# RWKV-6 attention and a Gelu MLP on one core: three of four additions into g made by accumulating transfers, with new slot plans

## The chip, the cores and the metric

The kernel runs on one core of a Trainium2 chip. The metric is device time in microseconds of one execution; several executions are taken, and their median stands for the kernel. A profile of one execution goes with it.

## The reference, cut to what matters

```python
# attention (rwkv6_finch): batch 4, heads 8, 768 steps, head size 48
for t in range(S):
    cur = einsum('bhd,bhe->bhde', u[None] * kt, vt)
    y[:, :, t] = einsum('bhd,bhde->bhe', rt, state + cur)
    state = wt[:, :, :, None] * state + einsum('bhd,bhe->bhde', kt, vt)
# MLP on x = y as (3072 tokens, 384)
h = x @ w_in                       # 384 -> 2048
g = 0.5 * h * (1 + erf(h / sqrt(2)))
out = g @ w_out                    # 2048 -> 384
```

Everything is f32. The weights arrive as 64-bit floats and are converted on the chip.

## The kernel before

The tokens are cut into eight blocks x = 0 to 7 of 384 tokens. For each block `attention(x, ...)` makes the 384 x 384 tile xT (features by tokens), and `mlp(x)` makes 384 rows of the output from it. The main loop runs eight turns: in turn x the MLP of block x - 1 is interleaved with the attention of block x (turn 0 has only attention, for two halves of the heads, and conversion of weights), and a last `mlp(7)` runs alone.

The order is written by hand through generators. Each stream yields between steps, and a string of `PLAN[x]` says which stream goes next: "." the MLP, "s" the attention, "f" the first step of the attention after it, "l" the loads of the next block (issued by SP), "c" the conversion of weights, "x" sums of xT, "w" masks and sums of weights, "p" preparation. All engines get their instructions in that order, and each engine runs its own in order; semaphores tie them together. In this way a long f32 matmul stream of the MLP keeps TensorE (PE) busy while VectorE (DVE), ScalarE (ACT) and DMAs work on the attention.

For x > 0 of the MLP, the product h = xT by w_in is made by `h_halves()` in a form with seven products of halves (as Strassen's and Winograd's scheme does) in place of eight. The hidden features go in HK = 4 turns q; each turn has the steps `first` to `seventh`. A step calls `two(o, q, ...)`, which issues two or four f32 matmuls of 128x192 into a PSUM bank (a matmul is two passes in the profile); `first`, `fifth` and `sixth` issue two, `second`, `third`, `fourth` and `seventh` four. What else they do:

- `first` copies its PSUM bank into a second one (L972, ACT), `second` goes on adding to the first.
- `second` and `fourth` end in a Gelu straight from PSUM (L961, ACT).
- `fifth` and `sixth` copy their PSUM into the tile g, for the quarters (1, 1) and (0, 1) of turn q (L992 and L996, ACT).
- `third` and `seventh` save their PSUM in the SBUF tile o_sb (L965, ACT; two buffers) and add it to what lies in g (L983 and L1001, DVE). A Gelu in place on g follows later (`gelu(q, 0, 1, ...)` and `gelu(q, 1, 1, ...)`; L961, for even blocks of the MLP L958 and L961, since 64 of the columns go to the tile `alone`).

The order in a turn q > 0 is first(q), third(q-1), seventh(q-1), second(q), fifth(q), sixth(q), fourth(q-1); after the last turn come seventh(3), third(3), and fourth(3) with the last Gelus, during the first product of the second matmul (`rest`). Then `of_g` (L921 to L925) makes sums of blocks of g on DVE, and `product` (L1068) multiplies by w_out in the same scheme.

Of the attention, the lines named later are L452 (products of k and r in blocks 0 and 1, PE), L505 and L494 (updates of r and k, DVE), L579 and L588 (the same products in later blocks), L711 (kv_ps, PE), L726 (the chain of states on DVE, which reads kv_ps), L752 (y_ps, PE), L897 (sums of xT), L385 (products of k and r on DVE), L163 and L204 (a memset of one column ahead of a load, so that the load waits for its buffer). GpSimd (POOL) sets up masks and tiles in the first microseconds and has no instruction of the kernel after that.

Of the kernel before, what the change touches and what calls it, by code (L numbers as in the profile page):

```python
# [18 lines left out]
ALU = mybir.AluOpType  # L19
# [17 lines left out]
NC_SP = 8  # L37
HALFWAY = 2
PLAN = {
    0: ".lls.....sslsc.lsslll.sl.sls..sl.lscsl..sss.lscs.lscs.s.clll.s..s.pcsss...wss..sccs.ffp",  # L40
    1: (
        "c.c.csc.cc.ccc.sscwllsc.cwccccs.wc.csscwc.cccc.s.slwccccc.ccs.cwc.ccw.cs.cscccccsccs.s..cc"
        "slcs.ccl.ss.lccsclccsc.lc.c..lwfws..ffwf.swf.f.xxw.x.f...lxx"
    ),
    2: (
        "w.ssws.l...swl.w.s.....ws....ssl.wwl.ws.slwsss.slsws..s.s......s.s.sss.s.ss...s..s...s..ls"
        "sl.lsfsff..s.flf...xx.fxfxx"
    ),
    3: (
        ".s...ls....s...s.ss...s.lsssss.s..ssls.ss...sss..ssssls.s...s...ls....lssl.slssl.fs..lffs."  # L50
        ".ffx.x..xxx"
    ),
    4: (
        "ss.ss...l.....ss..s..s...sss..ssss..ssll...ll.s.ss....sss....sss.ssl..s..s...s.ssll.s.lfsf"
        "..sf.ff..xx..xfxlx"
    ),
    5: (
        "ssl.s..l......ss.s..s...s.ssssss.s.s.s.ss...sss..lssslss.....ss.s.s....ls..lllssslfs..flsf"
        ".f..fx.x.xxx"
    ),  # L60
    6: (
        "ss....s...s.sls..s...s.l...sss.sllss..s.sss.l...s..s..ssslsss.s...ss....s....ss.lssl..lfsf"
        "f..fs..f.x.x.lxfxfx"
    ),
    7: ".s....s...s....sss...s.ssss.ssss.s..ss...sss..ssssss.s......s.s...s.s.sss..s..x..x.xxx",
}


# [5 lines left out]
def kernel(  # L74
# [9 lines left out]
    nc = tc.nc  # L84
# [32 lines left out]
    def bank_u(i):  # L117
        return pools["u"].tile([128, BANK], F32, name="u_ps", tag=f"u{i % 2}")

    def bank(name="o_ps"):  # L120
        return ps.tile([128, BANK], F32, name=name, tag="mm", bufs=2)
# [146 lines left out]
    for i, h in enumerate(QUARTERS[:1]):  # L268
        for a in range(3):
            w_q = (3 - a) * C // 4  # L270
            z = q_ints[1 if a == 0 else 2]
# [582 lines left out]
    HK = HF // 2  # L854
# [45 lines left out]
    def mlp(x):  # L900
# [14 lines left out]
        def of_g(k):  # L915

            s1.append(s12_of["s1"][k])
            s2.append(s12_of["s2"][k])
            s3.append(s3_sb[0][:, k * FG:(k + 1) * FG])
            a00, a10, a11 = (gs[g][:, :, a:a + 128] for g, a in ((k, 0), (k, 128), (k + 2, 128)))  # L920
            nc.vector.tensor_add(s1[k], a10, a11)  # L921
            yield
            nc.vector.tensor_sub(s2[k], s1[k], a00)
            yield
            nc.vector.tensor_sub(s3[k], a00, a10)  # L925
            yield

        def multiply(o, lhsT, rhs, start=False):
            nc.tensor.matmul(o, lhsT=lhsT, rhs=rhs, start=start, stop=True, skip_group_check=True)  # L929
# [3 lines left out]
        def h_halves():  # L933

            x00, t1, x10, x11, l0, l1 = (xT[:, c, b * HT:(b + 1) * HT] for c in range(3) for b in range(2))
            t2, t3, t4, l01 = x_sums

            def w(a, c):
                return lambda f: w_in_sb[:, (a * HF + f) // FI, c, f % FI * 128:(f % FI + 1) * 128]

            def s(i):
                return w(1, 0) if i == 1 else lambda f: s_of[i - 2][f // FI][:, f % FI * 128:(f % FI + 1) * 128]

            def two(o, q, *factors, start=False):
                for i in range(2):
                    for n, (lhs, rhs) in enumerate(factors):
                        multiply(o[:, i * HT:(i + 1) * HT], lhs(2 * q + i), rhs, start and i == n == 0)

            def of_two(o):
                return o.rearrange("p (f t) -> p f t", f=2)  # L950

            def g_of(q, a, b):
                return gs[2 * a + 2 * q // FG][:, 2 * q % FG:2 * q % FG + 2, b * HT:(b + 1) * HT]

            def gelu(q, a, b, z):
                o = g_of(q, a, b)
                if waits and b:
                    nc.scalar.activation(out=o[:, :, 0:256 - HT], in_=z[:, :, 0:256 - HT], func=AF.Gelu)  # L958
                    f = a * HF + 2 * q
                    o, z = alone[:, f:f + 2], z[:, :, 256 - HT:]  # L960
                nc.scalar.activation(out=o, in_=z, func=AF.Gelu)  # L961

            def saved(o):
                z = wk.tile([128, DM], F32, name="o_sb", bufs=2)
                nc.scalar.copy(out=z, in_=o)  # L965
                return of_two(z)

            def first(q):
                a_of[q] = h_bank()
                two(a_of[q], q, (w(0, 0), x00), start=True)  # L970
                u_of[q] = bank_u(q)[:, 0:2 * HT]
                nc.scalar.copy(out=u_of[q], in_=a_of[q])  # L972

            def second(q):
                two(a_of[q], q, (w(0, 1), x10), (w(0, 2), l0))
                gelu(q, 0, 0, of_two(a_of[q]))
                if q:
                    gelu(q - 1, 0, 1, g_of(q - 1, 0, 1))

            def third(q):  # L980
                two(z_of[q], q, (s(4), x11), (w(0, 2), l1))
                z = saved(z_of[q])
                nc.vector.tensor_add(g_of(q, 0, 1), g_of(q, 0, 1), z)  # L983

            def fourth(q):
                two(u_of[q], q, (w(1, 1), t4), (w(1, 2), l01))
                gelu(q, 1, 0, of_two(u_of[q]))

            def fifth(q):
                z_of[q] = h_bank()  # L990
                two(z_of[q], q, (s(1), t1), start=True)
                nc.scalar.copy(out=g_of(q, 1, 1), in_=of_two(z_of[q]))  # L992

            def sixth(q):
                two(u_of[q], q, (s(2), t2))
                nc.scalar.copy(out=g_of(q, 0, 1), in_=of_two(u_of[q]))  # L996

            def seventh(q):
                two(u_of[q], q, (s(3), t3), (w(1, 2), l1))
                z = saved(u_of[q])  # L1000
                nc.vector.tensor_add(g_of(q, 1, 1), g_of(q, 1, 1), z)  # L1001

            def h_bank():
                return bank("h_ps")[:, 0:2 * HT]

            a_of, z_of, u_of = {}, {}, {}
            for group in (0, 2, 1, 3):
                gs[group] = gp.tile([128, FG, T], F32, name="g")
            for q in range(HK):
                first(q)  # L1010
                yield
                if q:
                    third(q - 1)
                    yield
                    seventh(q - 1)
                    yield
                else:
                    fifth(q)
                    yield
                second(q)  # L1020
                yield
                if q:
                    fifth(q)
                    yield
                sixth(q)
                yield
                if q:
                    fourth(q - 1)
                    gelu(q - 1, 1, 1, g_of(q - 1, 1, 1))
                    yield  # L1030
            q = HK - 1
            seventh(q)
            yield
            third(q)
            for _ in of_g(0):
                pass
            yield

            def rest():
                fourth(q)  # L1040
                gelu(q, 0, 1, g_of(q, 0, 1))
                gelu(q, 1, 1, g_of(q, 1, 1))
            late[:] = [rest]
# [3 lines left out]
        if fast:  # L1047
            yield from h_halves()
# [47 lines left out]
        if halves:  # L1096
# [29 lines left out]
            for c in range(2):  # L1126
                z = o_sb[1][:, c * HM:(c + 1) * HM]
# [40 lines left out]
        elif ends:  # L1168
# [16 lines left out]
            for c in range(2):  # L1185
                z = o_sb[1][:, c * HM:(c + 1) * HM]
# [126 lines left out]
```

## Time and profile before

| | |
|---|---|
| median of 3 runs | 595.2 us (593.16 to 595.92) |
| profiled execution, its time | 593.95 us |
| profiled execution, its span | 592.2 us |
| PE, matmul | 573.1 us, 97% of the span |
| DVE | 443.9 us, 75% |
| ACT | 290.0 us, 49% |
| POOL | 8.0 us, 1% |
| HBM read and written | 36.24 and 4.72 MB |
| transfers of SP's and ACT's queue (q1) | 50,832 packets, 45.62 MB, 25.5% of 16 engines |
| additions into g on DVE (L983, L1001) | 56, 549 and 548 ns each |
| granted TensorE clock | 0.994 |

Times are in microseconds from the start of the span unless marked ns. The span runs from the first to the last instruction; the execution's own time is 1.75 us longer. A busy share is an average over stages; the attention's first block and the last MLP alone have other limits than the turns between. A line of the profile names the source line, the engine, the operation, the tiles (written <- read), the shape and the count.

### The profile page before, as it was taken

The page shows a single profiled execution, that of the slowest core. Times are in us where ns is not written, and L with a number is a line of the kernel's source. Part 1 is how long each engine was busy: PE and PEld are TensorE (multiplying, and loading weights), DVE is VectorE, ACT ScalarE, POOL GpSimd, SP SyncE. Part 2 cuts the span into 40 slices and gives each one's busy share as a digit, 9 for nine tenths or more (in the row PEclk, how much of TensorE's full clock was granted, in tenths as well). Part 3 has the DMA queues.
Part 4 walks back from the last instruction along what each step waited for, and adds up shares of the span by engine and source line. Part 5 has one row for each costly group of instructions (what it writes and reads, how often), then busy time and mean ns, then how long its engine had stood idle before and what let it go on. Part 6 is the DMA issues. An engine that isn't in the chain of part 4 may idle for free.

```text
span 592.2 us, 17602 instructions
## 1 busy us (share of the span) xinstructions
PE 573.1 (97%) x7602; PEld 522.3 (88%) x7616; DVE 443.9 (75%) x867; ACT 290.0 (49%) x668; POOL 8.0 (1%) x21
## 2 busy tenths in 40 slices
PE   6789999999999999999999999999999999999998
PEld 3576666699999999999999999999999999999997
DVE  6877976999959986787859987598859988521432
ACT  2259998235552556146552456345560467235400
POOL 3100000000000000000000000000000000000000
PEclk8989999999999999999999999999999999999999
DMA  6659652031032401431023301441013200110000
GB/s 236 201 192 311 226 186 85 19 120 56 1 65 68 130 5 34 116 122 37 2 43 103 121 19 22 112 138 55 1 32 92 72 2 12 31 45 1 1 14 34
DMA packets 51005, 46.82 MB, mean 79 GB/s; under 512 B 31728, under 2 KB 36080, under 8 KB 50928
## 3 DMA queue, kind: packets, MB, share of 16 engines
q1 hardware_dynamic: 50832, 45.62, 25.5%
q8 instruction: 60, 0.98, 0.7%
q14 instruction: 17, 0.14, 0.1%
q10 hardware_dynamic: 96, 0.07, 0.1%
HBM read 36.24 MB, written 4.72 MB: 69 GB/s over the span
## 4 chain that ended last, share of the span: by engine, by line
PE 62%; DVE 3%; SPq 1%; DMA 1%; issue 0%; ACT 0%; DVEq 0%
PE o_ps L1068 24%; PE h_ps L929 16%; PE u_ps L929 14%; PE d L588 4%; DVE st L726 2%; PE y_ps L752 1%; PE y_ps L797 1%; PE kv_ps L711 1%; SPq L531 1%; PE d L579 1%; DMA rkw<-in_rkw_dram 0%; DMA rkw<-kx 0%; DVE kx L385 0%; PE u_ps L588 0%; DVE f L1133 0%
## 5 line engine op out<-in xcount | busy, mean ns | idle before, releaser
L929 PE MATMUL h_ps<-xT,w_in_sb 128*128 128x192 f32 x560 | 111.0, 330 | 0.1
L929 PEld LDWEIGHTS h_ps<-xT,w_in_sb 128*128 128x128 f32 x560 | 93.0, 190 | 3.7 <-ACT g L961 1.4
L929 PE MATMUL u_ps<-s,w_in_sb 128*128 128x192 f32 x224 | 41.1, 326 | 0.0
L1068 PE MATMUL o_ps<-w_out_sb,g 128*128 128x192 f32 x224 | 39.8, 326 | 0.0
L929 PEld LDWEIGHTS u_ps<-s,w_in_sb 128*128 128x128 f32 x224 | 37.1, 190 | 0.1
L1068 PEld LDWEIGHTS o_ps<-w_out_sb,g 128*128 128x128 f32 x224 | 37.0, 190 | 0.0
L604 ACT COPY a_sb<-d 32x256 f32<-32x256 f32 (+8 forms) x90 | 32.7, 363 | 4.0 <-PE d L588 2.5
L726 DVE SCALAR_TENSOR_TENSOR st<-st,tot_sb,kv_ps 128x48 f32<-128x48 f32 x160 | 29.1, 258 | 5.3 <-PE kv_ps L711 5.2
L452 PEld LDWEIGHTS d<-rkw 64*64 64x64 f32 x1152 | 19.5, 137 | 15.3 <-issue 9.3
L1054 PE MATMUL h_ps<-xT,w_in_sb 128*128 128x384 f32 x96 | 32.6, 492 | 0.0
L823 ACT COPY ysb<-y_ps 128x384 f32<-128x384 f32 x8 | 3.8, 480 | 57.8 <-PE y_ps L797 28.8
L1068 PE MATMUL o_ps<-w_out_sb,f 128*128 128x192 f32 x176 | 32.0, 330 | 0.0
L1068 PE MATMUL o_ps<-t,e 128*128 128x192 f32 x176 | 31.2, 328 | 0.0
L1068 PE MATMUL o_ps<-w_out_sb,e 128*128 128x192 f32 x176 | 31.2, 328 | 0.0
L1068 PE MATMUL o_ps<-t,s 128*128 128x192 f32 x176 | 31.2, 328 | 0.0
L983 DVE TENSOR_TENSOR g<-g,o_sb 128x384 f32<-128x384 f32 x28 | 15.4, 549 | 20.9 <-ACT o_sb L965 20.9
L1068 PE MATMUL o_ps<-t,g 128*128 128x192 f32 x176 | 31.0, 330 | 0.0
L452 PE MATMUL d<-rkw 64*64 64x64 f32 (+1 forms) x1152 | 22.2, 224 | 7.5 <-DMA rkw<-in_rkw_dram 3.0
L1068 PEld LDWEIGHTS o_ps<-w_out_sb,f 128*128 128x128 f32 x176 | 28.7, 190 | 0.4
L1068 PEld LDWEIGHTS o_ps<-t,g 128*128 128x128 f32 x176 | 28.6, 190 | 0.5
L1068 PEld LDWEIGHTS o_ps<-t,e 128*128 128x128 f32 x176 | 28.8, 190 | 0.2
L1068 PEld LDWEIGHTS o_ps<-t,s 128*128 128x128 f32 x176 | 28.8, 190 | 0.2
(163 smaller groups left out, 1187.4 us busy)
## 6 DMA issues: line engine op xcount, KB each, us to landing
rkw<-in_rkw_dram SPq DMA_DIRECT2D x54, 256.0 KB, 3.7
raw<-in_w_out_dram SPq DMA_DIRECT2D x8, 768.0 KB, 4.8
v_in<-in_v_dram SPq DMA_DIRECT2D x8, 584.0 KB, 4.3
raw<-in_w_in_dram SPq DMA_DIRECT2D x5, 768.0 KB, 6.6
out_dram<-o_sb SPq DMA_DIRECT2D x20, 192.0 KB, 1.9
rkw<-kx SPq DMA_DIRECT2D x72, 48.0 KB, 2.0
rkw<-in_rkw_dram SPq DMA_DIRECT2D x6, 384.0 KB, 5.7
raw<-in_w_in_dram SPq DMA_DIRECT2D x9, 256.0 KB, 4.7
```

Of the source, the lines that this page charges most:

```text
L452: nc.tensor.matmul(d[half[p], g, n * width:(n + 1) * width], lhsT=kc[half[g], b, i, p], rhs=right(half[g], b, i, p), start=True, stop=True)
L531: dma.dma_start(out=block_of_kt(dst, src), in_=kb[src * 32:(src + 1) * 32, dst])
L579: nc.tensor.matmul(fine_of(d, g)[half[p], a * n_b:], lhsT=places[half[g], a, p * C:(p + 1) * C], rhs=fine_sb[half[g], 0:FINE - a, a], star ...
L588: nc.tensor.matmul(o[half[p], i * 3 * C // 2:(i + 1) * 3 * C // 2], lhsT=kc[half[g], n // NI, n % NI, p], rhs=rx[half[g], 2 * n + p], star ...
L604: nc.scalar.copy(out=at[z, g, first:behind, (a + 1) * h:], in_=d[z, :, :, to] if g == slice(None) else d[z, :, to])
L711: nc.tensor.matmul(kv_ps[half[g], p, i * D:(i + 1) * D], lhsT=k_t(b, i, p, g), rhs=vs(b, i, g)[half[p], 0:D], start=True, stop=True)
L726: nc.vector.scalar_tensor_tensor(out=stq[:, q, c], in0=stq[:, q, c - 1] if c else b4[:, q, NC - 1], scalar=totq[:, q, c:c + 1], in1=kvs[q ...
L752: nc.tensor.matmul(y[p][half[g ^ swap(b)], i * C:(i + 1) * C], lhsT=vs(b, i, g)[half[p]], rhs=at[half[p], g, b * NI + i, :], start=(i == 0 ...
L929: nc.tensor.matmul(o, lhsT=lhsT, rhs=rhs, start=start, stop=True, skip_group_check=True)
L983: nc.vector.tensor_add(g_of(q, 0, 1), g_of(q, 0, 1), z)
L1054: nc.tensor.matmul(h_ps, lhsT=w_in_sb[:, f // FI, j, f % FI * 128:(f % FI + 1) * 128], rhs=xT[:, j, :], start=(j == 0), stop=(j == NJ - 1))
L1068: nc.tensor.matmul(o, lhsT=lhs(j), rhs=rhs(j), start=start and j == 0, stop=(j == HF - 1), skip_group_check=True)
```

## The change

Three things are changed. First, for the turns q = 0, 1 and 2 of `h_halves` the addition of o_sb to g is no longer a DVE instruction but a DMA from o_sb to g with an accumulating operation, issued by GpSimd; for q = 3 DVE adds as before. With seven blocks in this form these are 42 transfers (128 partitions, two rows of 192 f32 each, 192 KB) and 14 additions. Second, the Gelus of these quarters are issued later: `gelu(q-1, 0, 1)` moves from second(q) to behind fourth(q-1), and `gelu(q-1, 1, 1)` from behind fourth(q-1) to behind third(q) of the next turn, or behind seventh(3) after the last. Third, all eight strings of `PLAN` are new; they hold other orders of the same streams. Below, two of the eight strings are shown.

```diff
 PLAN = {
-    0: ".lls.....sslsc.lsslll.sl.sls..sl.lscsl..sss.lscs.lscs.s.clll.s..s.pcsss...wss..sccs.ffp",
+    0: ".s...sl.ll.lclsllllssssl.lsl.l.ssl.lls..ssssc..s.sclcs.s..s..s.s.ss.s..csps.s.s.fpcfw",
...
-    7: ".s....s...s....sss...s.ssss.ssss.s..ss...sss..ssssss.s......s.s...s.s.sss..s..x..x.xxx",
+    7: "ss.ss.....s..s..s....s.ssss.ss...ss.s.ss..sss..sssss..s..s...s..s..s.s.sss..s.x..x..xxx",
 }
...
             def second(q):
                 two(a_of[q], q, (w(0, 1), x10), (w(0, 2), l0))
                 gelu(q, 0, 0, of_two(a_of[q]))
-                if q:
-                    gelu(q - 1, 0, 1, g_of(q - 1, 0, 1))
+
+            def add_to(q, z, g):
+                if q < HK - 1:
+                    nc.gpsimd.dma_start(out=g, in_=z, accum_op=ALU.add)
+                else:
+                    nc.vector.tensor_add(g, g, z)
 
             def third(q):
                 two(z_of[q], q, (s(4), x11), (w(0, 2), l1))
-                z = saved(z_of[q])
-                nc.vector.tensor_add(g_of(q, 0, 1), g_of(q, 0, 1), z)
+                add_to(q, saved(z_of[q]), g_of(q, 0, 1))
...
             def seventh(q):
                 two(u_of[q], q, (s(3), t3), (w(1, 2), l1))
-                z = saved(u_of[q])
-                nc.vector.tensor_add(g_of(q, 1, 1), g_of(q, 1, 1), z)
+                add_to(q, saved(u_of[q]), g_of(q, 1, 1))
...
                 if q:
                     third(q - 1)
+                    if q > 1:
+                        gelu(q - 2, 1, 1, g_of(q - 2, 1, 1))
                     yield
                     seventh(q - 1)
                     yield
...
                 if q:
                     fourth(q - 1)
-                    gelu(q - 1, 1, 1, g_of(q - 1, 1, 1))
+                    gelu(q - 1, 0, 1, g_of(q - 1, 0, 1))
                     yield
             q = HK - 1
             seventh(q)
+            gelu(q - 1, 1, 1, g_of(q - 1, 1, 1))
             yield
             third(q)
```

More of the change, by code (lines that the diff above doesn't have):

```diff
@@ L39 @@
 PLAN = {
-    0: ".lls.....sslsc.lsslll.sl.sls..sl.lscsl..sss.lscs.lscs.s.clll.s..s.pcsss...wss..sccs.ffp",
+    0: ".s...sl.ll.lclsllllssssl.lsl.l.ssl.lls..ssssc..s.sclcs.s..s..s.s.ss.s..csps.s.s.fpcfw",
     1: (
-        "c.c.csc.cc.ccc.sscwllsc.cwccccs.wc.csscwc.cccc.s.slwccccc.ccs.cwc.ccw.cs.cscccccsccs.s..cc"
-        "slcs.ccl.ss.lccsclccsc.lc.c..lwfws..ffwf.swf.f.xxw.x.f...lxx"
-    ),
-    2: (
-        "w.ssws.l...swl.w.s.....ws....ssl.wwl.ws.slwsss.slsws..s.s......s.s.sss.s.ss...s..s...s..ls"
-        "sl.lsfsff..s.flf...xx.fxfxx"
-    ),
-    3: (
-        ".s...ls....s...s.ss...s.lsssss.s..ssls.ss...sss..ssssls.s...s...ls....lssl.slssl.fs..lffs."
-        ".ffx.x..xxx"
-    ),
-    4: (
-        "ss.ss...l.....ss..s..s...sss..ssss..ssll...ll.s.ss....sss....sss.ssl..s..s...s.ssll.s.lfsf"
-        "..sf.ff..xx..xfxlx"
-    ),
-    5: (
-        "ssl.s..l......ss.s..s...s.ssssss.s.s.s.ss...sss..lssslss.....ss.s.s....ls..lllssslfs..flsf"
-        ".f..fx.x.xxx"
-    ),
-    6: (
-        "ss....s...s.sls..s...s.l...sss.sllss..s.sss.l...s..s..ssslsss.s...ss....s....ss.lssl..lfsf"
-        "f..fs..f.x.x.lxfxfx"
+        "cs.c.cc.sslclcc.cs..ccswcc.sswccc.cccs.c.cccss.ccc.sc.scwlcclcsc.css.cs.clscsscclccc.sclls"
+        "lc.wcc.ccfcccf.cc.s...fc.wcc.swcc.cc...cf.w.wwwx.xwxf.wl.f.xx"
+    ),
+    2: (
+        "sw..sl..wss.....s..sws....ssw.wsw.sw.w.ss.lss..s.sw.ll.sw.s...ssls.s.s.ls..ss.s....s...sss"
+        ".lsll.f.s.fs.ff..x.xl.xfxx"
+    ),
+    3: (
+        "l.s.s..s...sls.ss....s...s.sss.ss.ss.ss...s.ssss..sssssssll....s....l..sl.sssls..llsf..sf."
+        "ff.x.l.x.xfxx"
+    ),
+    4: (
+        "sss...s..l....sl.s..s.s...l.ss..sss.l.s.s.ss.s.s...s.sl.ssl...sssss..s.....s.s..lss.sllfsf"
+        "..lfs.f.f.x.x.xfxx"
+    ),
+    5: (
+        ".ss...sss.l.....ss....sl.sssslss.s......sslss.sss..sssss..s..sl..s..s...s.lslsll.ssf.ff.s."
+        ".x..x.lxxx"
+    ),
+    6: (
+        "lls...ssss.s.s.s......l.s.s....s..sss.ssss.ss..sll..s...s..s..sss.s.sl.ss..s....slss.sl.lf"
+        ".sf.f.s.ff..xx.xfxlx"
     ),
-    7: ".s....s...s....sss...s.ssss.ssss.s..ss...sss..ssssss.s......s.s...s.s.sss..s..x..x.xxx",
+    7: "ss.ss.....s..s..s....s.ssss.ss...ss.s.ss..sss..sssss..s..s...s..s..s.s.sss..s.x..x..xxx",
 }
```

## The prediction

> **What bounds the kernel now.** I read the page's first two parts, the engines' busy time by stage, the waits of TensorE, the waits of all engines, ACT's and PE's timeline in one turn of the loop that is edited, and the DMA issues. The page first:
>
> ```profile
> PE 573.1 (97%) x7602; PEld 522.3 (88%) x7616; DVE 443.9 (75%) x867; ACT 290.0 (49%) x668; POOL 8.0 (1%) x21
> ```
>
> PE is the bound. A busy PE need not be a dense one, so I also looked at the pitch: in the timeline 12 passes of 128x192 take 1.95 us, 0.1625 us each, in all stages after 50 us. A tighter order has nothing to win there; only idle time can go. By stage (columns: stretch, its length, then busy time of PE, PEld, DVE, ACT, POOL, the clock, the DMA share, GB/s):
>
> ```profile
> 0.00:50.00 50.00, 37.36 (x1089) 27.19 (x1102) 36.92 (x113) 21.80 (x37) 8.02 (x21) 0.93 0.66 213
> ...
> 258.00:330.00 72.00, 71.63 (x871) 69.12 (x869) 59.12 (x113) 33.16 (x83) 0.00 (x0) 1.00 0.20 53
> 330.00:394.00 64.00, 63.67 (x832) 60.80 (x832) 51.90 (x97) 32.54 (x84) 0.00 (x0) 1.00 0.28 79
> ```
>
> In the two loops shown PE idles 0.37 and 0.33 us; of the 19.1 us of idle time in the span 12.6 lie in the first 50 us. DVE is busy for 52 to 59 us of those loops, but that is work beside PE. Which waits does it end? The waits of PE, in full for all that matters:
>
> ```profile
> PE d L452 <- DMA rkw<-in_rkw_dram: 3.0, 1, 3.0
> PE d L452 <- issue: 2.3, 2, 1.5
> PE warm L225 <- ACT zeros L217: 2.3, 1, 2.3
> PE y_ps L752 <- DVE st L726: 2.1, 5, 0.7
> PE kv_ps L711 <- issue: 2.0, 1, 2.0
> PE kv_ps L711 <- ACT kx L687: 1.1, 2, 0.9
> PE d L452 <- DVE rkw L505: 0.7, 1, 0.7
> PE d L452 <- DVE rkw L163: 0.4, 1, 0.4
> PE warm L225 <- issue: 0.3, 1, 0.3
> PE u_ps L929 <- DVE s L897: 0.3, 1, 0.3
> PE warm L225 <- DVE raw L204: 0.2, 1, 0.2
> ```
>
> Waits that DVE ends are 2.1 + 0.7 + 0.4 + 0.3 + 0.2 = 3.7 us. That is all that a freer DVE and better slots can give back, unless they also shorten a wait that no instruction of the program ends ("issue").
>
> **What is removed.** 42 of the 56 additions on DVE:
>
> ```profile
> L983 DVE TENSOR_TENSOR g<-g,o_sb 128x384 f32<-128x384 f32 x28 | 15.4, 549 | 20.9 <-ACT o_sb L965 20.9
> L1001 DVE TENSOR_TENSOR g<-g,o_sb 128x384 f32<-128x384 f32 x28 | 15.3, 548 | 7.1 <-ACT o_sb L965 6.9
> ```
>
> 42 x 0.549 = 23.1 us of DVE work, six additions or 3.3 us in each of seven loops. The row's last part says that DVE stood idle for 28 us ahead of them, so it had the time. On the path it is worth little: the largest wait that DVE ends, y_ps behind the state chain of L726 (2.1 us), comes after matmuls that make kv_ps, and DVE itself waits for these ("DVE st L726 <- PE kv_ps L711", 5.2 us in 8 waits). The chain of 16 or 20 such operations starts when kv_ps is there, however free DVE was before. I keep those 2.1 us, and the 0.3 of the x sums.
>
> **What is moved.** All loops have other slots. The matmuls are the same in kind and count (3,840 in both programs, two passes each where f32), and in both orders PE changes 122 times between 64-row and 128-row tiles, so PE's work is the same sum. In loop 0 the first instructions of the weight and x loads (the one-column memsets of L163 and L204) stand in other places of DVE's order: five of L163 now stand together ahead of the second updates. I count the waits of loop 0 behind L505 and L163 (0.7 + 0.4) as gone, 1.0 us rounded. In loop 1 the attention's matmuls come some slots earlier and the Gelu products later; PE is 99% busy there (70.98 of 72 us) with either first. SP's loads move with the slots; DMA share is 0.2 to 0.28 in the later loops, so I cost that at nothing; were a load late, the attention's first step would wait, with 3.7 us for a 256 KB load as its measure.
>
> **What is added.** 42 transfers of 192 KB that add o_sb to g, issued from POOL, which has nothing after 50 us. POOL waits for ACT's copy into o_sb, and nothing else is queued behind it but the next transfer. The one that waits for the landing is ACT, at the Gelu, and behind it stand ACT's copies that PE needs. So the edit stands or falls with the time from the copy's end to the Gelu. One turn, ACT alone (start, length):
>
> ```profile
> 335.04 0.48 ACT L965 COPY o_sb<-h_ps 128x384 f32<-128x384 f32 x1 [0.84 <-PE h_ps L929]
> 336.33 0.48 ACT L965 COPY o_sb<-u_ps 128x384 f32<-128x384 f32 x1 [0.82 <-PE u_ps L929]
> ...
> 338.15 0.31 ACT L958 ACTIVATE g<-g 128x128 f32<-128x128 f32 x1
> ...
> 340.24 0.50 ACT L961 ACTIVATE g<-u_ps 128x384 f32<-128x384 f32 x1 [0.72 <-PE u_ps L929]
> 340.62 0.30 ACT L958 ACTIVATE g<-g 128x128 f32<-128x128 f32 x1
> 340.82 0.41 ACT L961 ACTIVATE rkw<-g 128x256 f32<-128x256 f32 x1
> 341.13 0.48 ACT L972 COPY u_ps<-h_ps 128x384 f32<-128x384 f32 x1
> ```
>
> Before, the Gelu of the first sum came at 338.15, 2.6 us after its copy ended (335.52). Now it stands behind fourth()'s Gelu, where 340.62 is now: a window of 340.62 - 335.52 = 5.1 us. The second sum's Gelu moves behind the next third(): from the end of seventh()'s matmuls 36 passes (second 8, fifth 4, sixth 4, fourth 8, first 4, third 8) x 0.1625 = 5.9 us, its window also about 5.9 us, since a copy stands at each end. Where slots of the attention lie between, it is longer by up to 1 us a burst. If a landing is late by less than some reserve, ACT waits and PE does not: the copy at 341.13 ends at 341.61 and is first needed by second() of the next turn, which PE starts at 343.29. That is 1.6 us of reserve, so PE loses time from 5.1 + 1.6 = 6.7 us on. It then loses up to 1 us per us in each of 21 turns (three of four, seven loops).
>
> How long is a transfer? Nothing in this trace adds in flight, so from both sides:
>
> ```profile
> rkw<-in_rkw_dram SPq DMA_DIRECT2D x54, 256.0 KB, 3.7
> ...
> out_dram<-o_sb SPq DMA_DIRECT2D x20, 192.0 KB, 1.9
> rkw<-kx SPq DMA_DIRECT2D x72, 48.0 KB, 2.0
> rkw<-in_rkw_dram SPq DMA_DIRECT2D x6, 384.0 KB, 5.7
> ```
>
> Low end: 1.9 us, the plain store of 192 KB from the same tile. High end: 9.1 us, the slowest single load of the trace, in the crowded start. An addition reads both operands, 384 KB, and writes 192 KB, so I place it between the 256 KB and the 384 KB load: (3.7 + 5.7) / 2 = 4.7 us, an estimate. That is inside 5.1, by 0.4 us for ACT and by 2.0 us for PE. Two come 1.3 us apart, and the second has 0.8 us more of window. On this value the transfers cost nothing; what hides them is those 32 to 36 passes. Their load on the DMA engines (24 MB over 430 us, 56 GB/s beside some 60) leaves room.
>
> The Trainium skill, "DMA: Bandwidth & Descriptors", section on the anatomy of one DMA on GpSimd's path, fits 2.0 us plus bytes over 436 GB/s; by that (an estimate) a transfer takes 2.45 us and the sum is the same. No run here shows such a transfer yet.
>
> **Sum.** Removed DVE work 0, loop 0 -1.0, transfers 0: -1.0 us. The profiled execution took 593.95 us (span 592.2 and 1.75 around it); its forecast is 592.95. It lies 1.25 us under the median of the three runs, 595.2, so on the median I forecast 594.2. Differences under 0.5% (3 us) are about what a measurement of this kernel cannot tell from no change.
>
> **Rivals.**
> Late landing (slower). The place is ACT's wait at the moved Gelu, the price 21 turns x (L - 6.7 us), the point from which it decides 6.7 us. For it: reads and write one behind the other would be 5.7 + 1.9 = 7.6 us, hence 21 x 0.9 = 19 us and 613 us; at the high end, 9.1, it is 50 us and 644. Against it: a 192 KB store lands in 1.9, and most loads of 256 KB in 3.7. Chance 0.30.
>
> Descriptors held up by DVE (slower). POOL must make the transfer's descriptors while DVE works 80% of the time. If a DVE operation could shut POOL out, the longest here (L385, 2.2 us) makes 4.7 + 2.2 = 6.9 us, 0.2 us over in at most 21 turns: 4 us, 598.4. Against it: POOL is empty after 50 us, so the trace cannot show it, and most DVE operations last under 1 us. Chance 0.06. The Trainium skill, "SBUF — State Buffer", section on who interferes with whom, says that an operation of DVE in a two-port mode blocks GpSimd fully and starves its descriptor making, and names copies and tensor_scalar as those that can. By that rule little is at stake: the copies in these loops (L731) take 0.25 us.
>
> All DVE waits go (faster). If slots and a freer DVE clear all 3.7 us: 591.5; with the "issue" wait of 2.3 us in loop 0 gone too, 589.2. For it: a new order of loop 0 shifts the loads that fill the DMA engines there (share 0.66). Against it: the kv_ps argument above. Chance 0.21.
>
> **How the numbers follow.** Forecast 0.43 (its own range 592.2 to 597.5, one wait more or less), late landing 0.30, descriptors 0.06, faster 0.21. So faster by over 0.5% 0.21, within 0.43, slower 0.36. The range: low 590.0, under which I leave 0.05 (the "issue" wait gone too); high 613, which leaves out the half of the late landings that are over 7.6 us, 0.15.
>
> **What would show it.** Right: POOL's transfers land within 5.1 us of ACT's copy; no row of ACT at L961 or L958 waits for g<-o_sb; PE busy 573 us as before; DVE about 421 us; the y_ps waits behind L726 still near 2 us. Wrong: waits of ACT for those transfers, and behind them PE at second() (h_ps, L929) waiting for ACT's L972; then the late landing holds, and its length gives the price. A gain over 3 us would have to show as PE idle time missing from the first 50 us or from y_ps.

## The result and the profile after

The changed kernel takes 593.1 us (median of 22 runs, 591.35 to 594.94), the kernel before 595.3 us beside it (22 runs, 592.68 to 597.25). The ratio is 0.9966, 95% interval 0.9952 to 0.998: faster by about 0.3%, 2.0 us. That is clear of no change, and inside the bound of 0.5%. The profiled execution took 592.35 us, with a span of 590.5, against 593.95 and 592.2 before; 592.95 was forecast for it.

The busy times of the changed kernel, from the first part of its page:

```profile
PE 573.7 (97%) x7616; PEld 521.3 (88%) x7616; DVE 424.3 (72%) x825; ACT 290.8 (49%) x668; POOL 58.7 (10%) x63
```

PE's work is what it was (573.1). DVE lost 19.6 us, and POOL took on 50.7. By stage, with the columns as before:

```profile
0.00:50.00 50.00, 39.10 (x1192) 26.89 (x1193) 37.90 (x112) 21.41 (x36) 7.99 (x21) 0.93 0.60 197
258.00:330.00 72.00, 71.62 (x871) 69.16 (x870) 58.61 (x108) 33.83 (x85) 7.20 (x6) 1.00 0.36 84
330.00:394.00 64.00, 63.67 (x835) 60.94 (x834) 46.55 (x90) 32.39 (x84) 7.23 (x6) 1.00 0.36 77
```

In the two loops PE idles 0.38 and 0.33 us, as before (0.37 and 0.33), although DVE is freer by up to 5 us and the DMA share went from 0.20 and 0.28 to 0.36. There was nothing to win and nothing was lost. The waits of PE in the changed kernel, those that stand for or replace rows of before:

```profile
PE d L452 <- issue: 3.2, 2, 2.3
...
PE kv_ps L711 <- issue: 1.5, 1, 1.5
PE y_ps L752 <- DVE st L726: 1.3, 4, 0.4
PE h_ps L929 <- DVE o_sb L1196: 0.7, 1, 0.7
PE d L588 <- DVE kx L563: 0.6, 1, 0.6
PE kv_ps L711 <- ACT kx L687: 0.6, 2, 0.3
PE y_ps L797 <- DVE fence L762: 0.5, 1, 0.5
PE d L452 <- DVE rkw L494: 0.2, 1, 0.2
```

Waits that DVE ends are 1.3 + 0.7 + 0.6 + 0.5 + 0.2 = 3.3 us, where they were 3.7. The waits behind L505 and L163 are gone (1.1 us), and L494 (0.2) and 0.9 more of "issue" at L452 stand in their place. At kv_ps the two rows went from 3.1 to 2.1 us. No wait of PE leads to a transfer. The transfers themselves, from the page's costliest groups and DMA issues, and from the view of line L980 (who waited for it):

```profile
L980 POOL DMA_DIRECT2D g<-o_sb x42 | 50.7, 1250 | 482.0 <-ACT o_sb L965 473.4
...
g<-o_sb POOLq DMA_DIRECT2D x42, 192.0 KB, 3.6
...
  ACT g L961: 0.2, 1
```

POOL needs 1.2 us to issue one, and from the issue's start to the landing it is 3.6 us (median; 3.4 to 5.4). ACT waited for one of 42, for 0.2 us. One turn of ACT shows why:

```profile
333.66 0.48 ACT L965 COPY o_sb<-h_ps 128x384 f32<-128x384 f32 x1 [0.84 <-PE h_ps L929]
334.96 0.48 ACT L965 COPY o_sb<-u_ps 128x384 f32<-128x384 f32 x1 [0.82 <-PE u_ps L929]
...
339.65 1.34 ACT L557 COPY kx<-rkw 128x384 f32<-128x384 f32 x3 [1.55 <-DVE rkw L419]
340.89 0.48 ACT L961 ACTIVATE g<-u_ps 128x384 f32<-128x384 f32 x1
341.28 0.30 ACT L958 ACTIVATE g<-g 128x128 f32<-128x128 f32 x1
```

The first copy ends at 334.14, POOL issues at 334.44 (0.30 us later, the median of the 42; 0.63 at most), the sum lies in g at 338.97, 4.5 us after that (one of the slower landings), and its Gelu starts at 341.28. In this turn copies of the attention (L557), which stand in ACT's queue ahead of fourth()'s Gelu and wait for DVE, widen the window to 7.1 us. Over all turns the window from the copy's end to the Gelu is 4.6 to 7.8 us for first sums and 5.2 to 9.4 us for second sums, and the landing comes 3.7 to 5.6 us after the copy's end. The slowest landing is longer than the shortest window; they fell in different turns.

Where did the 1.6 us of span come from? The start of each block's first `h_halves` matmul cuts the trace into stages. Loop i is the stretch from the start of block i-1's MLP to that of block i's; the last stage is the last MLP. Lengths less those of before, in us, for the changed kernel and all experiments below:

| kernel | loops 0, 1 | 2 | 3 | 4 | 5 | 6 | 7 | last MLP |
|---|---|---|---|---|---|---|---|---|
| changed | -0.75 | -0.70 | +0.07 | 0.00 | -0.38 | -0.44 | +0.50 | +0.08 |
| new slots alone | +0.1 | -0.70 | +1.58 | +1.05 | +6.41 | +5.61 | +1.72 | 0 |
| no transfers | -0.2 | -0.65 | +1.67 | +1.12 | +3.76 | +5.38 | +2.15 | 0 |
| old slots | +0.3 | -0.36 | -0.17 | -0.01 | +0.11 | 0 | -0.17 | +0.07 |
| new slots 0 to 2 | -1.3 | -0.71 | +1.10 | 0 | +0.02 | 0 | 0 | 0 |
| early Gelus | +0.8 | +0.64 | +0.91 | +0.70 | +1.41 | -0.44 | +1.16 | +2.10 |
| two of half the size | -1.0 | -0.70 | +0.04 | 0 | -0.38 | +0.04 | +0.51 | +0.06 |
| four of four | +3.0 | -0.70 | +2.09 | +0.32 | 0 | -0.15 | +0.90 | +0.89 |
| moved first | +2.5 | +3.02 | +0.07 | +1.45 | -0.38 | -0.44 | +0.74 | +0.42 |

The first transfer stands at 127.8 us, in loop 2. What happens in the first column can't come from transfers. The eight kernels with the new strings have the same instructions there, and one profile of each lies between -1.3 us ("new slots 0 to 2") and +3.0 us ("four of four"), so a span is compared with care and the columns behind it are read first.

So the gain of the changed kernel's profile lies in loops 0 to 2 (-1.45 us), and loops 3 to 7, with 30 of the 42 transfers, give -0.25 together. Of the -1.45, what stands in every profile with the new strings is one wait of PE in loop 1 (kv_ps behind L687, from 0.9 to 0.3 us) and one in loop 2: y_ps behind L726, 0.74 us long before (it ends at 181.2 us) and gone after, is the -0.70 of the table. The rest is within the scatter of the first column.

### The profile page after: what moved, and what is told of

Its sections match the earlier page's. It is cut to its first block, busy times and chain, and to the rows that moved or that the text cites. A ratio compares the mean times of both kernels' runs of the same rounds, so it can differ in the third digit from the quotient of the medians.

```text
span 590.5 us, 17675 instructions
## 1 busy us (share of the span) xinstructions
PE 573.7 (97%) x7616; PEld 521.3 (88%) x7616; DVE 424.3 (72%) x825; ACT 290.8 (49%) x668; POOL 58.7 (10%) x63
## 3 DMA queue, kind: packets, MB, share of 16 engines
q0 software_dynamic: 11424, 8.26, 10.7%
## 5 line engine op out<-in xcount | busy, mean ns | idle before, releaser
L980 POOL DMA_DIRECT2D g<-o_sb x42 | 50.7, 1250 | 482.0 <-ACT o_sb L965 473.4
L452 PEld LDWEIGHTS d<-rkw 64*64 64x64 f32 x1152 | 20.0, 142 | 16.1 <-issue 13.1
L726 DVE SCALAR_TENSOR_TENSOR st<-st,tot_sb,kv_ps 128x48 f32<-128x48 f32 x160 | 29.0, 257 | 3.8 <-PE kv_ps L711 3.7
L621 DVE COPY_PREDICATED a_sb<-quarter,d 128x480 f32<-128x480 uint8 (+5 forms) x54 | 23.1, 439 | 10.4 <-PE d L588 9.2
L1073 PEld LDWEIGHTS o_ps<-w_out_sb,e 128*128 128x128 f32 x176 | 28.8, 190 | 0.2
```

Source lines behind the costliest of these rows:

```text
L452: nc.tensor.matmul(d[half[p], g, n * width:(n + 1) * width], lhsT=kc[half[g], b, i, p], rhs=right(half[g], b, i, p), start=True, stop=True)
L621: nc.vector.copy_predicated(out=an[:, :, :, :, (a + 1) * h:], mask=mask.to_broadcast(data.shape), data=data)
L726: nc.vector.scalar_tensor_tensor(out=stq[:, q, c], in0=stq[:, q, c - 1] if c else b4[:, q, NC - 1], scalar=totq[:, q, c:c + 1], in1=kvs[q ...
L980: nc.gpsimd.dma_start(out=g, in_=z, accum_op=ALU.add)
L1073: nc.tensor.matmul(o, lhsT=lhs(j), rhs=rhs(j), start=start and j == 0, stop=(j == HF - 1), skip_group_check=True)
```

## The experiments

The forecast rested on one theory: DVE has time ahead of its additions, so removing them is worth nothing, the new slots alone would do as well, and the transfers are hidden by the later Gelus. The rival, formed from the result: the new slots are denser for DVE and hold only because the additions are gone, so each part alone costs and together they cancel.

**New slots alone.** The kernel before, with all eight new strings; additions on DVE, Gelus in their old places.

```diff
 PLAN = {
-    0: ".lls.....sslsc.lsslll.sl.sls..sl.lscsl..sss.lscs.lscs.s.clll.s..s.pcsss...wss..sccs.ffp",
+    0: ".s...sl.ll.lclsllllssssl.lsl.l.ssl.lls..ssssc..s.sclcs.s..s..s.s.ss.s..csps.s.s.fpcfw",
...
```

> The kernel before with the eight new slot strings only: additions on DVE, Gelus in their old places. Theory A (the additions on DVE are off the path, the gain of 2 us is the new slots' own): 593 to 594 us, y_ps waits of PE behind L726 down to 1.3 us as in the changed kernel. Theory B (the new slots are drawn for a DVE that is 23 us freer and overrun it when the additions are back): slower than before, by 5 to 15 us, with new waits of PE or ACT that DVE ends in the loops from 122 us on.

Measured: 609.2 us (606.62 to 610.31), ratio 1.0245 (1.0212 to 1.0278); span 607.9. Loops 0 to 2 keep their gain, and loops 3 to 7 lose 16.4 us. DVE and PE in loop 5, from the timelines of this kernel (start, length):

```profile
353.37 0.96 DVE L563 TENSOR_TENSOR kx<-kx,tot_sb 128x768 f32<-128x768 f32 x1
356.09 0.56 DVE L983 TENSOR_TENSOR g<-g,o_sb 128x384 f32<-128x384 f32 x1 [1.75 <-ACT o_sb L965]
357.39 0.56 DVE L1001 TENSOR_TENSOR g<-g,o_sb 128x384 f32<-128x384 f32 x1 [0.74 <-ACT o_sb L965]
357.86 2.18 DVE L621 COPY_PREDICATED a_sb<-quarter,d 128x480 f32<-128x480 uint8 x5
...
362.29 1.88 PE L588 MATMUL d<-kx,rkw 64*64 64x96 f32 x40 [1.73 <-DVE a_sb L671]
```

The same steps in the changed kernel, from its timelines:

```profile
348.94 0.96 DVE L563 TENSOR_TENSOR kx<-kx,tot_sb 128x768 f32<-128x768 f32 x1
349.81 2.45 DVE L621 COPY_PREDICATED a_sb<-quarter,d 128x480 f32<-128x480 uint8 x6
...
354.27 1.88 PE L588 MATMUL d<-kx,rkw 64*64 64x96 f32 x80
```

The additions cost 0.56 us of work each, and in front of them DVE stands 1.75 + 0.74 = 2.5 us, because it works in order and the next thing in its queue is an addition whose o_sb isn't there. Behind it is the attention's masking (L621), which starts 3.5 us after L563 ends, and PE then waits 1.73 us for what follows from that. In the changed kernel L621 starts when L563 ends, and PE doesn't wait. Idle time ahead of an instruction, which the prediction read as spare time, is here the damage itself: the queue behind is ready and can't pass.

There is a second path. In loop 6, near 414 us, an addition comes late behind the attention's work on DVE, ACT waits 3.3 us for it at the early Gelu, and PE waits 1.5 us for the copy that stands behind that Gelu (L992).

The idle PE paid a second time here. The same kernel by stretches of 1 us (the clock is the third number from the end):

```profile
361.00:362.00 1.00, 0.00 (x0) 0.00 (x0) 1.00 (x2) 0.00 (x0) 0.00 (x0) 0.91 0.00 0
362.00:363.00 1.00, 0.71 (x19) 0.71 (x23) 1.00 (x2) 0.65 (x2) 0.00 (x0) 0.50 0.00 0
...
367.00:368.00 1.00, 1.00 (x5) 0.79 (x3) 0.00 (x0) 0.00 (x0) 0.00 (x0) 0.50 0.00 0
368.00:369.00 1.00, 1.00 (x18) 0.65 (x17) 0.00 (x0) 0.66 (x3) 0.00 (x0) 0.67 0.00 0
```

From 361.8 to 368.7 the granted clock is one half, which costs 3.4 us of matmul time; that is over half of what loop 5 lost. The Trainium skill, "TensorE: Matmul & The Clock Gate", section "Part 1: The HAM clock gate", says that a gate halves the clock after an idle window of some 3.4 us and frees it after a busy one. The trace agrees on the half and on the length (about 6.8 us, two such windows), but here PE had been idle for at most 1.73 us at a stretch, and for 2.4 us (0.71 and 1.73) of the 4.3 us before 362.3. When the clock fell, at 361.8, PE had been idle for 2.0 of the last 3.4 us. This second price is not certain: in the next experiment PE has the same two stalls in the same place (0.71 us before 359.8, 1.73 before 362.6), and its clock stays whole there.

**No transfers.** The changed kernel with all 56 additions on DVE, Gelus late.

```diff
             def add_to(q, z, g):
-                if q < HK - 1:
+                if False:
                     nc.gpsimd.dma_start(out=g, in_=z, accum_op=ALU.add)
```

> The changed kernel with all 56 additions on DVE again; new slots and late Gelus stay. Theory A: as the changed kernel, 593 us. Theory B: slower than before by 5 to 15 us; a little better than the new slots alone, since the late Gelus leave DVE 2.6 us more for each addition before ACT waits.

Measured: 607.1 us (604.4 to 608.13), ratio 1.0211 (1.0174 to 1.0248); span 605.4. PE's waits in this kernel:

```profile
PE d L579 <- DVE a_sb L621: 2.8, 3, 1.8
PE d L588 <- DVE kx L563: 2.7, 3, 1.5
PE d L588 <- DVE a_sb L671: 2.6, 3, 1.7
```

These are the attention's products behind DVE's masking and scaling, and of the three only L563 has a wait in the changed kernel (0.6). Late Gelus repair little of it: 14.1 us are lost in loops 3 to 7 instead of 16.4, and of the 2.3 us between them 1.7 are the clock's. One half-clock stretch of 3.4 us follows an idle time of 1.76 us in loop 6, which is 1.7 us of the 5.4 here, against 3.4 us with the new slots alone. The additions are all that sets this kernel apart from the changed one, so it shows that the new slots of loops 3 to 7 need the additions off DVE's queue.

**Old slots.** The changed kernel, transfers and late Gelus in it, with all eight old strings.

```diff
 PLAN = {
-    0: ".s...sl.ll.lclsllllssssl.lsl.l.ssl.lls..ssssc..s.sclcs.s..s..s.s.ss.s..csps.s.s.fpcfw",
+    0: ".lls.....sslsc.lsslll.sl.sls..sl.lscsl..sss.lscs.lscs.s.clll.s..s.pcsss...wss..sccs.ffp",
...
```

> The changed kernel's transfers and late Gelus with the eight old slot strings. Both theories: within 1 us of before (595.3), as DVE's 23 us were off the path in the old order: the y_ps waits behind L726 stay at about 2 us. If the freed DVE by itself shortened the path: 593 us or less. No ACT wait for a landing, since windows are 5 us and a landing takes 3.6.

Measured: 593.3 us (592.12 to 597.63), ratio 0.9997 (0.9975 to 1.0019); span 591.9. Transfers and late Gelus are worth nothing in the old slots, and cost nothing. No stage moved by 0.4 us. PE's waits at y_ps behind L726 are 1.9 us (2.1 before), which bears out that this chain doesn't care how free DVE is, and the landing is again 3.6 us. So of the rival's two parts only the slots cost when they stand alone.

**New slots 0 to 2.** The kernel before with the new strings of loops 0 to 2, the old ones from loop 3 on, and two attention steps put ahead of loop 3's string, since the new ones leave two more to it.

```diff
     3: (
-        ".s...ls....s...s.ss...s.lsssss.s..ssls.ss...sss..ssssls.s...s...ls....lssl.slssl.fs..lffs."
+        "ss.s...ls....s...s.ss...s.lsssss.s..ssls.ss...sss..ssssls.s...s...ls....lssl.slssl.fs..lffs."
```

> The kernel before (additions on DVE, old Gelus) with the new strings for loops 0, 1 and 2 only, and old ones from loop 3 on (two more attention steps at the head of loop 3, to have as many in all). In the traces the whole gain in span lies between 43 and 185 us, in loops 1 and 2, where only six transfers are made. If it belongs to the slots of these loops: 593 to 594 us, y2 of loop 2 (first L797) about 1.5 us earlier than before. If it needs the freed DVE there: 595 or more, the first L797 of loop 2 not earlier.

Measured: 594.1 us (593.04 to 595.28), ratio 0.9997 (0.998 to 1.0015); span 591.3. Loops 0 to 2 of its profile gain 2.0 us without any transfer; the 0.71 of loop 2 are from slots alone, and of the 1.3 us in the first column most is within its scatter. Loop 3 gives 1.1 us back, with one wait of PE at L588 behind DVE's L563 of 1.5 us, and no gain is left in the runs. With the new slots alone and with no transfers the same wait stands in the same place, 1.5 us, and in the changed kernel it is 0.6. So the two steps put ahead aren't needed for it, and the additions on DVE are the likelier reason; that was not taken apart.

**Early Gelus.** The changed kernel with the Gelus in their old places.

```diff
             def second(q):
                 ...
+                if q:
+                    gelu(q - 1, 0, 1, g_of(q - 1, 0, 1))
...
-                    if q > 1:
-                        gelu(q - 2, 1, 1, g_of(q - 2, 1, 1))
...
-                    gelu(q - 1, 0, 1, g_of(q - 1, 0, 1))
+                    gelu(q - 1, 1, 1, g_of(q - 1, 1, 1))
```

> The changed kernel (transfers, new slots) with the Gelus back in their early places. A transfer lands 3.6 us after its issue and 0.3 us after the copy it is issued; the early window is 2.6 us for the first sum and 3.8 us for the second, so ACT waits about 1.3 us for each first sum, some 20 waits and 25 us in all. Theory A (prediction's reserve of 1.6 us between ACT's lateness and PE's loss): no loss, 593 us. Theory B (ACT's copies behind the early Gelu are needed sooner than those behind the late one): PE loses a part of each wait, 3 to 10 us, and the late Gelus are what makes the transfers free.

Measured: 601.4 us (598.86 to 602.93), ratio 1.0111 (1.0083 to 1.0139); span 599.4, 8.9 us over the changed kernel's, of which 1.5 lie before the first transfer and 7.4 behind it. ACT's waits:

```profile
ACT g L961 <- DMA g<-o_sb: 19.0, 12, 2.8
...
ACT g L958 <- DMA g<-o_sb: 14.8, 9, 3.1
```

21 waits of 0.9 to 3.1 us, 33.8 in all, and PE loses 7.4 of them. What each wait has beyond the prediction's reserve of 1.6 us adds up to 5.8 us. The later Gelus are what hides the transfers.

**Two of half the size.** Each sum of the changed kernel added by two transfers of 96 KB, one row of 192 each.

```diff
-                    nc.gpsimd.dma_start(out=g, in_=z, accum_op=ALU.add)
+                    for i in range(2):
+                        nc.gpsimd.dma_start(out=g[:, i], in_=z[:, i], accum_op=ALU.add)
```

> The changed kernel with each addition as two transfers of 96 KB (one per 192-column row of g), 84 in all. POOL's issue of 1.2 us is per transfer (theory A): the second sum's last half is issued 1.3 to 2.4 us later and lands at its window's end; ACT waits in a few turns, under 1 us each, time within 1 us of the changed kernel. If the issue time goes by bytes or rows (theory B): a half is issued in 0.6 us and nothing at all changes.

Measured: 592.6 us (591.77 to 595.18), ratio 0.9967 (0.9948 to 0.9985); span 590.8. The records of a pair overlap on POOL: the second issue starts some 0.54 us after the first, whose record takes 0.86 us (median of those with none ahead), where an issue of twice the size takes 1.20; the second's takes 1.21 beside the first. So neither theory holds as it stands: an issue of half the size is shorter, and two of them follow each other more closely than their records are long. Each lands in 3.0 us (median). From the copy's end to the landing of the second half it is 3.7 us for first sums and 4.5 for second sums (medians), where the whole one took 3.8 and 4.2. ACT waits once, for 0.2 us. There is room in the window; the size is not what decides.

**Four of four.** The changed kernel with the additions of q = 3 as transfers too, 56 in all.

```diff
-                if q < HK - 1:
+                if True:
                     nc.gpsimd.dma_start(out=g, in_=z, accum_op=ALU.add)
```

> The changed kernel with the last turn's additions as transfers too, 56 in all and none on DVE; their Gelus stay in rest(), where the window from the copy's end is about 2.5 us. ACT waits for a landing in each of seven loops, 1.4 us, 10 us in all. With the reserve of 1.6 us: PE loses under 2 us in all, time 593 to 595. If the product that follows needs these Gelus at once: 7 x 1.4 = 10 us more, 603.

Measured: 599.6 us (596.78 to 600.31), ratio 1.0072 (1.0046 to 1.0099); span 598.5, of which 3.8 us over the changed kernel lie before the first transfer and 4.2 behind it. ACT waits for 7 landings, 13.6 us in all, up to 3.6, and PE waits for those Gelus at the second matmul (o_ps, 1.8 and 0.5 us). Behind third(3), the last of the order, only fourth(3) and the first product stand, so these transfers have less beside them. The price is real, but less than the waits' sum.

**Moved first.** In the changed kernel the first sum of a turn (third's) is copied onto itself by a GpSimd transfer before the one that adds, so that its landing comes later by a known amount.

```diff
-            def add_to(q, z, g):
+            def add_to(q, z, g, twice=False):
                 if q < HK - 1:
+                    if twice:
+                        nc.gpsimd.dma_start(out=z, in_=z)
                     nc.gpsimd.dma_start(out=g, in_=z, accum_op=ALU.add)
...
-                add_to(q, saved(z_of[q]), g_of(q, 0, 1))
+                add_to(q, saved(z_of[q]), g_of(q, 0, 1), True)
```

> The changed kernel with landings made late on purpose: each first sum's o_sb is first copied onto itself by a transfer of GpSimd's queue, and the addition is issued when that has landed, so 0.3 + about 3 + 3.6 = 7 us lie between the copy and the landing; the second sum's transfer queues behind. The prediction's price, 21 turns x (L - 6.7 us): with 7 us 6 us slower than the changed kernel, with 7.5 us 17 us; ACT waits of about 2 us in each turn without slots of the attention. If lateness of ACT costs PE nothing (rival): 593 us.

Measured: 601.7 us (598.55 to 603.01), ratio 1.0109 (1.0069 to 1.015); span 599.6. Its DMA issues, and the PE wait that it adds:

```profile
g<-o_sb POOLq DMA_DIRECT2D x42, 192.0 KB, 4.1
...
o_sb<-o_sb POOLq DMA_DIRECT2D x21, 192.0 KB, 2.2
...
PE h_ps L929 <- ACT u_ps L972: 2.7, 1, 2.7
```

From the copy's end to the landing it is now 6.7 us in the median for the first sum (6.3 to 9.0), and 6.9 us for the second, whose transfer queues behind (6.4 to 8.7). ACT waits 18 times, 28.3 us in all, up to 3.3, and PE's longest new wait is the one that the late-landing rival named: second() behind the copy of L972. 3.3 us of the 9.1 us of extra span lie before the first transfer, 5.7 behind it. What each ACT wait has beyond 1.6 us adds up to 7.2 us. So the place of the late landing holds, and the size of its reserve about. The median of 6.7 us stands at the point from which the prediction counted a loss, and the kernel loses all the same, since landings scatter: 11 of the 21 first sums land later than 6.7 us. Their excess adds up to 9.9 us, which the prediction would price at up to as much; 5.7 were lost.

## Why the prediction was right, and where it was not

**The total.** -1.0 us was forecast on the profiled execution and -1.6 measured; -2.0 by the ratio of the runs. The forecast's case, a change within 0.5%, held. That the size came near is in part luck, as the terms below show.

**PE and DVE.** PE's 573 us stayed (573.7). DVE came to 424.3 and not to 421: the removed work is 23.1 us, the busy time fell by 19.6. Added up record by record, DVE's instructions did fall by 23.1 us (from 496.0 to 472.8). The busy time counts a stretch in which two records overlap once, and such overlap went from 52.1 to 48.6 us: part of each addition had lain under its neighbours.

**Removed DVE work at nothing.** Right for the old order, and shown by the old slots. The reason given for it (y_ps waits for a chain that starts at kv_ps) held there too, 1.9 us. Wrong as a statement about this change: without the removal the same slots cost 14.1 to 16.4 us in loops 3 to 7 (12.4 to 13.0 without the half clock). The step that failed is the reading of DVE's 28 us of idle time ahead of L983 and L1001 as room. It is time in which DVE's queue stood in order behind a copy of ACT; whether that hurts depends on what the slots put behind it. The removal bought the slots of loops 3 to 7, and these bought 0.25 us.

**Loop 0 at -1.0.** The waits behind L505 and L163 went, as counted, but loop 0 did not get shorter. Its first y products (L797), first before and then in the changed kernel:

```profile
39.22 4.14 PE L797 MATMUL y_ps<-rkw,st 64*64 64x64 f32 x78
```

```profile
40.14 1.33 PE L797 MATMUL y_ps<-rkw,st 64*64 64x64 f32 x40
41.99 1.32 PE L797 MATMUL y_ps<-rkw,st 64*64 64x64 f32 x38 [0.52 <-DVE fence L762]
```

They start 0.9 us later in the changed kernel: "issue" at L452 rose from 2.3 to 3.2 us, and a stretch at half clock (0.50 from 26.6 to 30.0 us, worth up to 1.7 us) lies ahead of them. Both runs of 78 still end near 43.3 us, since the kernel before has its half clock just there, from 39.9 to 43.3 us. With the old slots in the changed code they start at 40.00, and in the other kernels with the new strings at 39.6 to 43.2, so this start scatters by more than the forecast gain. The size of the total came out near because the slots of loops 1 and 2 gave what wasn't counted: 0.6 us at kv_ps behind ACT's L687 (loop 1), and 0.7 at y_ps behind L726 (loop 2), where 2.1 was to stay. That is one wait of five; the other four, 0.3 us each, stand in the changed kernel as before. So the claim that y_ps doesn't depend on the slots held in four loops of five. The 0.5 at L797 doesn't replace it: it stands in loop 0, with the old slots in the changed code too.

**Transfers at nothing.** Right, with a term mis-sized: 4.7 us was estimated for a landing and 3.6 measured, so the margin to the window of 5.1 us, less 0.3 until the issue, is 1.2 and not 0.4. The shortest windows were 4.6 and 5.2 us, where 5.1 and 5.9 were put down for the two sums. The estimate placed an addition between the loads of 256 and 384 KB; the plain GpSimd transfer of the same 192 KB takes 2.2, and the addition 1.4 more, of which 0.6 is the issue (1.20 us against 0.58). The load on the DMA engines was over-counted: the trace has 8.26 MB for the 42 transfers, and 24 was put down. By the fit of the Trainium skill, "DMA: Bandwidth & Descriptors", section on the anatomy of one DMA on GpSimd's path, 2.45 us (an estimate) was to be expected; the trace has 3.6, and the plain one, at 2.2, is what comes near it. That the window is needed is shown by the early Gelus: with the old one, 2.6 us for the first sum, ACT waits 21 times.

**The rivals.** Late landing did not come, since 3.6 us from the issue (5.4 at most), or 5.6 at most from the copy's end, stays under 6.7; where it was made to come, it came in the place named. Descriptors held up by DVE: POOL's issues take 1.20 us in the median and 1.63 at most beside a DVE that is busy for 72% of the time, and all over 1.33 us started before the issue ahead of them had ended. L642 on DVE takes 1352 ns with a POOL issue beside it and 1350 without (medians). No hold-up shows here. All DVE waits go: 3.3 of 3.7 us are still there.

## What to carry to other kernels

Idle time of an engine in front of an instruction is room only if nothing ready stands behind it in the same queue, so a change of order that leans on an engine, and the relief of that engine, have to be priced together: here the relief alone is worth 0, the order alone +15 us, and both give -2. A transfer put in place of an engine's work is free as long as its slowest landing, not its median, fits between the producer's end and the consumer's turn in its own queue, or misses it by less than the reserve behind the consumer; move the consumer first, and count that reserve. When PE is the bound, a stall of under 2 us can cost more than its length: two of eleven did here.

## What the runs showed of the hardware

An accumulating transfer of 192 KB from SBUF to SBUF takes 3.6 us from issue to landing, the plain one of the same size from the same queue 2.2 (medians). The issue on GpSimd takes 1.20 us for the accumulating one, 0.58 for the plain one, and 0.86 for an accumulating one of 96 KB with none ahead of it.

A stall of PE of 1.7 us, alone (in the kernel without transfers) or behind a shorter one (with the new slots alone), went with a stretch of 3.4 or some 6.8 us at a granted clock of 0.50, that is 1.7 or 3.4 us of matmul time more. It doesn't always: the ten traces have eleven stalls of 1.4 to 2.7 us behind the first 50 us, and nine left the clock whole, the longest one too. What tells them apart stays open.

Such stretches stand in the first 50 us of most of these traces, in other places: between 9 and 13 and between 39 and 44 us before, between 9 and 13 and between 26 and 31 in the changed kernel, between 27 and 34 in the one that moves first, and in none with the old slots in the changed code. They don't explain why equal instructions start the second stage at different times: the changed kernel lost up to 3.4 us to them there and the one with four of four up to 1.7, and the changed one was still earlier, by 3.8 us. Of that difference, 1.4 us are "issue" waits at L452 (3.2 and 4.6) and 1.0 a later load (2.9 and 3.9); what sets these stays open, and with it how much of the gain in the first column is the change's.
